# The last product of a float32 chain by seven products of halves within each group of 504 tokens, in place of eight; its output copies all on ScalarE; a new written order

## The chip, the core and the metric

The kernel runs on one core of one Trainium2 chip. The time is the device time of one execution in microseconds (us), the median of the runs. The five engines are TensorE (PE in the rows; its weight loads are shown apart as PEld), VectorE (DVE), ScalarE (ACT), GpSimd (POOL) and SyncE (SP), whose queue issues nearly all DMAs.

## What is computed

Attention over 4 batches of 576 positions and 8 heads, as a sum of a pooled part and a part within a band of 7 positions, gives x (2304 tokens by 512). Two feed-forward stages follow:

```python
def _moe_ref(x, w1, w2, w3, w_out):
    a = x @ w1
    b = x @ w2
    h = a * b @ w3
    return (h @ w_out).astype(np.float32)

def _moe2_ref(x, w1, w2, w3, w_out):
    h = np.maximum(np.maximum(x @ w1, x @ w2), x @ w3)
    return (h @ w_out).astype(np.float32)
```

The change is to the very last product, `h @ w_out` of the second stage: h has 768 features, the output 512.

## The kernel before

**Number format.** Every large product is made three times in the one-pass 32-bit format `fp32r`: both operands are split into a high part (a cast on ScalarE) and a low part (a subtraction on VectorE, `split`, L444 and L446), and `mm3` (L451 to L453) adds low by high, high by low and high by high into one PSUM bank. The product of w3 and w_out (`pw`, L740) is made once in plain float32, ahead of everything.

**Tokens.** The 2304 tokens are cut into four chunks of N = 504 and a rest of 288. Tokens lie in the columns of the moving operand, features in the partitions.

**Stages.** First attention (`down`, `slab`) and the product of weights, mixed; then the first feed-forward stage (`front`, `back`), whose result y goes to DRAM. Then nine units (three pairs of feature blocks by three weight matrices) of the second stage: `halves_front` makes, for two chunks side by side (a group G of 1008 tokens), the product of 2 by 2 blocks with seven products instead of eight (sums of the operands are made ahead by `sums_of_x` and `convert`), keeps the running maximum in `zb` and `area`, and `rest_front` does the 288 tokens plainly. After the third weight matrix the maximum goes to `g_dram[f]`, one array for each of the six feature blocks f.

**The last product.** `final(ch, ...)` loads the six blocks of a chunk (`g_dram`), splits each (`gg`), and makes for each of four output blocks l one PSUM tile by 6 x 3 matmuls of the chunk's width: 72 matmuls a chunk, of 504 columns in four chunks and of 288 in the rest, which comes last. The weights `wm` are three tiles of 1 MB, fetched from `m_dram`. Each PSUM tile is scattered into output tiles by small copies (L1010), half on VectorE and half on ScalarE. An output tile (384 columns) holds one block l of a third of two batches; when its last copy is done, it is sent (192 KB, `out`).

**What sets the order.** Nothing is scheduled at run time. `Program.add` gives every step a number with its dependences; `ORDER` lists for every engine the numbers in the order in which that engine issues them, and the steps are written out so. An engine that waits holds back all that stands behind it in its list. SP's list holds the DMAs: one that waits holds back the others.

Of the kernel before, what the change touches and what calls it, by code (L numbers as in the profile page):

```python
# [96 lines left out]
    "DVE":  # L97
# [38 lines left out]
    "ACT":  # L136
# [231 lines left out]
def attention_moe_kernel(ctx, tc, q0, k0, v0, mask0, ql, kl, vl, mask, qkp, vp, w12, w3t, wo, m123, mo, out):  # L368
# [428 lines left out]
    y_dram = [outside([P, B * S], F32, f"y_dram{l}") for l in range(KX)]  # L797
    g_dram = [outside([P, B * S], F32, f"g_dram{f}") for f in range(NF2)]
    w_dram = [[outside([P, 2048], F32, f"w_dram{u}_{i}") for i in range(2)] for u in range(3 * NF2 // 2)]
    m_dram = [outside([P, 2048], F32, f"m_dram{i}") for i in range(NF2 // 2)]  # L800

# [425 lines left out]
```

## Time and profile before

| what | us |
|---|---|
| median of 3 runs | 756.32 |
| lowest, highest | 754.67, 760.01 |
| the profiled execution | 757.28 |
| its span in the trace | 755.5 |
| TensorE busy in the span | 728.2 |
| VectorE busy | 472.8 |
| ScalarE busy | 315.8 |

The sum of the prediction is made on the profiled execution, which took 0.96 us more than the median of the runs, and 1.8 us more than the span that its trace shows.

### The profile page before, as it was taken

The page shows a single profiled execution, that of the slowest core. Times are in us where ns is not written, and L with a number is a line of the kernel's source. Part 1 is how long each engine was busy: PE and PEld are TensorE (multiplying, and loading weights), DVE is VectorE, ACT ScalarE, POOL GpSimd, SP SyncE. Part 2 cuts the span into 40 slices and gives each one's busy share as a digit, 9 for nine tenths or more (in the row PEclk, how much of TensorE's full clock was granted, in tenths as well). Part 3 has the DMA queues.
Part 4 walks back from the last instruction along what each step waited for, and adds up shares of the span by engine and source line. Part 5 has one row for each costly group of instructions (what it writes and reads, how often), then busy time and mean ns, then how long its engine had stood idle before and what let it go on. Part 6 is the DMA issues. An engine that isn't in the chain of part 4 may idle for free.

```text
span 755.5 us, 15650 instructions
## 1 busy us (share of the span) xinstructions
PE 728.2 (96%) x6404; PEld 572.8 (76%) x6404; DVE 472.8 (63%) x859; ACT 315.8 (42%) x704; POOL 48.3 (6%) x114
## 2 busy tenths in 40 slices
PE   3998999999999999999999999999999999999997
PEld 1445467777877778777888899878887888888886
DVE  5999997776334632343277699978855663475322
ACT  6755495655625743421335356432221220214412
POOL 3210020103020210000000000000000000000000
PEclk9997999999999999999999999999999999999999
DMA  9989565023431331113267586867884265554425
GB/s 322 301 228 306 149 174 152 14 72 78 112 91 44 91 61 34 39 45 101 85 224 262 196 284 243 279 235 276 306 281 147 91 245 198 217 181 145 128 89 198
DMA packets 63191, 126.99 MB, mean 168 GB/s; under 512 B 23376, under 2 KB 43856, under 8 KB 60432
## 3 DMA queue, kind: packets, MB, share of 16 engines
q1 hardware_dynamic: 58512, 122.45, 48.6%
q0 software_dynamic: 4608, 3.55, 3.3%
q8 instruction: 50, 0.82, 0.4%
q14 instruction: 21, 0.17, 0.1%
HBM read 87.43 MB, written 38.54 MB: 167 GB/s over the span
## 4 chain that ended last, share of the span: by engine, by line
PE 86%; DVE 6%; DMA 5%; issue 2%; ACT 0%; SPq 0%; ACTq 0%; DVEq 0%
PE pb L451 11%; PE pb L452 11%; PE pb L453 10%; PE pf L451 9%; PE pf L453 9%; PE pf L452 9%; PE py L451 5%; PE pw L740 5%; PE py L452 4%; PE py L453 4%; PE poq L678 3%; PE sq L633 2%; DMA raw<-w3t 2%; DMA wu<-w_dram 1%; PE po L579 1%
## 5 line engine op out<-in xcount | busy, mean ns | idle before, releaser
L451 PE MATMUL pb<-xc,wu 128*128 128x504 f32 (+1 forms) x324 | 120.7, 373 | 3.1 <-ACT t L906 1.7
L451 PE MATMUL pf<-xt,w 128*128 128x504 f32 (+1 forms) x320 | 120.3, 376 | 0.0
L453 PE MATMUL pb<-xc,wu 128*128 128x504 f32 (+1 forms) x324 | 119.7, 370 | 0.0
L452 PE MATMUL pb<-xc,wu 128*128 128x504 f32 (+1 forms) x324 | 119.7, 369 | 0.0
L452 PE MATMUL pf<-xt,w 128*128 128x504 f32 (+1 forms) x320 | 118.9, 372 | 0.0
L453 PE MATMUL pf<-xt,w 128*128 128x504 f32 (+1 forms) x320 | 118.9, 371 | 0.0
L451 PEld LDWEIGHTS pb<-xc,wu 128*128 128x128 f32 x324 | 60.8, 188 | 17.8 <-DVE t L904 4.3
L451 PEld LDWEIGHTS pf<-xt,w 128*128 128x128 f32 x320 | 60.1, 188 | 11.6 <-ACT dp L572 1.1
L740 PE MATMUL pw<-wf 128*128 128x512 f32 x128 | 64.2, 652 | 4.6 <-DVE wf L477 4.6
L453 PEld LDWEIGHTS pb<-xc,wu 128*128 128x128 f32 x324 | 60.9, 188 | 10.1
L452 PEld LDWEIGHTS pb<-xc,wu 128*128 128x128 f32 x324 | 60.9, 188 | 9.8
L453 PEld LDWEIGHTS pf<-xt,w 128*128 128x128 f32 x320 | 60.1, 188 | 10.3
L452 PEld LDWEIGHTS pf<-xt,w 128*128 128x128 f32 x320 | 60.2, 188 | 9.9
L904 DVE TENSOR_TENSOR t<-t,pb 128x504 f32<-128x504 f32 x60 | 40.4, 677 | 41.7 <-PE pb L453 28.2
L906 ACT COPY t<-pb 128x504 f32<-128x504 f32 x36 | 20.9, 582 | 105.9 <-PE pb L453 102.2
L451 PE MATMUL py<-g,wp 128*128 128x504 f32 (+1 forms) x160 | 64.0, 400 | 0.0
L452 PE MATMUL py<-g,wp 128*128 128x504 f32 (+1 forms) x160 | 59.5, 372 | 0.0
L453 PE MATMUL py<-g,wp 128*128 128x504 f32 (+1 forms) x160 | 59.5, 372 | 0.0
L772 DVE TENSOR_TENSOR z<-pf,z 128x504 f32<-128x504 f32 (+1 forms) x40 | 25.4, 636 | 49.9 <-PE pf L453 38.6
L740 PEld LDWEIGHTS pw<-wf 128*128 128x128 f32 x128 | 25.4, 208 | 33.7 <-issue 27.1
L452 PE MATMUL pb<-gg,wm 128*128 128x504 f32 (+1 forms) x120 | 44.6, 372 | 0.0
L451 PE MATMUL pb<-gg,wm 128*128 128x504 f32 (+1 forms) x120 | 44.4, 370 | 0.0
(117 smaller groups left out, 1191.0 us busy)
## 6 DMA issues: line engine op xcount, KB each, us to landing
wu<-w_dram SPq DMA_DIRECT2D x18, 1024.0 KB, 7.8
w_dram<-hl SPq DMA_DIRECT2D x20, 512.0 KB, 4.7
qk<-qkp SPq DMA_DIRECT2D x16, 576.0 KB, 4.3
raw<-m SPq DMA_DIRECT2D x18, 512.0 KB, 3.8
raw<-w3t SPq DMA_DIRECT2D x16, 512.0 KB, 8.2
raw<-w SPq DMA_DIRECT2D x16, 512.0 KB, 7.2
w_dram<-hls SPq DMA_DIRECT2D x16, 512.0 KB, 4.1
area<-g_dram SPq DMA_DIRECT2D x24, 252.0 KB, 2.7
```

Of the source, the lines that this page charges most:

```text
L451: nc.tensor.matmul(o, wlo, xhi, start=first, stop=False, skip_group_check=again)
L452: nc.tensor.matmul(o, whi, xlo, start=False, stop=False, skip_group_check=again)
L453: nc.tensor.matmul(o, whi, xhi, start=False, stop=last, skip_group_check=again)
L579: e.matmul(po()[a * D:(a + 1) * D, :GD], vd()[:, k, a * D:(a + 1) * D], pt()[:, k, a], start=(k == 0), stop=(k == 1),)
L633: e.matmul(sps[a]()[j * 32:(j + 1) * 32, (half * HP + hp) * BK:(half * HP + hp + 1) * BK], q[h, t:t + 32], k[h, t:t + BK], start=True, sto ...
L678: e.matmul(pos[hp]()[a * D:(a + 1) * D, i * BQ:(i + 1) * BQ], vw()[h, a, i], pt().rearrange("p a n -> p (a n)")[h, c:c + BQ], start=True, ...
L740: e.matmul(os[i](), w()[:, i * P:(i + 1) * P], o(), start=n == 0, stop=n == NF - 1)
L772: prog.add(psum(n), lambda e, pp=pp: e.tensor_tensor(z()[:, :n], pp()[:, :n], z()[:, :n], op=ALU.mult), [pp], [z])
L904: prog.add(dve(N), lambda e: e.tensor_tensor(ap(o), ap(x), ap(y), op=op), [x, y], [o])
L906: copy = lambda o, x: prog.add(act(N), lambda e: e.copy(ap(o), ap(x)), [x], [o])
```

## The change

For each of the four chunks of 504 tokens, `final` now takes the chunk as two halves of 252 columns, the six feature blocks as two halves of three, and the four output blocks as two halves of two, and makes the 2 by 2 block product with seven products. A product has 2 x 3 x 3 = 18 matmuls of 252 columns, so a chunk has 126. Six sums of operands are needed: four are made of g in every chunk, on VectorE (L1029 of the changed kernel), and those of the weights once in `convert`; seven operands of 756 columns are split for each chunk (`go`), and five additions of 504 columns (L1054) and two copies (L1056) put the products together. So `m_dram` and `wm` double to six tiles of 1 MB. The rest of 288 tokens is still made plainly, but ahead of the four chunks (`final_rest`), and in the ninth unit `rest_front` comes ahead of the two groups. Output tiles now hold two blocks l (384 KB each, 12 instead of 24), and all copies into them are on ScalarE (`put`, L982). All five lists of `ORDER` are new.

```diff
-    "12 307 21 23 308 39 116 309 25 310 117 48 50 66 311 312 52 77 75 93 313 79 127 314 151 104 102 152 106 129 "
+    "12 307 23 21 116 39 308 309 25 310 117 50 48 66 311 312 52 75 77 93 79 313 127 151 104 314 102 152 106 129 "
...
-    def convert(srcs, sums, hl, to):
+    def convert(srcs, blocks, hl, to):
...
-        two = [(cv, to[0])]
-        if sums:
-            sm = cvr.tile([P, 1024], F32, "cv")
...
+        sm = cvr.tile([P, 1024], F32, "cv")
+        a11, a12, a21, a22 = ((cv, i) for i in blocks)
...
+    def put(src, t0, n, ls, stride):
+
+        runs = {}
+        for m in range(t0 // TT, (t0 + n) // TT):
...
+        for (b, s, h), (u0, i0, ni) in runs.items():
...
+            prog.add(("ACT", 0.09 + 0.0019 * len(ls) * ni * TT), lambda e, o=o[0], u0=u0, i0=i0, ni=ni, b2=b2, odd=odd: e.copy(
+                view(o(), ls[0] % 2 * T + b2 * NC + 2 * i0 + odd, [[T, len(ls)], [2, ni], [BC, TT]]),
+                view(src(), u0 * TT, [[stride, len(ls)], [2 * TT, ni], [1, TT]])), [src], [(o[0], (b, s, h, i0, ls[0]))])
+            if o[1] == 2 * T:
+                dma(lambda rd=rd, j=j, h=key[2]: out[rd * NJ + j, 2 * h:2 * h + 2].rearrange("l p t -> p l t"),
+                    lambda o=o[0]: o(), [o[0]], [], P * T * 8)
...
-                    cost = (act if h else dve)(ni * TT)
-                    prog.add(cost, lambda e, h=h, o=o[0], c0=c0, ni=ni, b2=b2, i0=i0, odd=odd, pp=pp: (e.copy if h else e.tensor_copy)(
...
+    def final(ch, stage, ops, temps, ms):
+        prog.group += 1
+        n = N // 2
+        b1x, b2x = (stage.tile([P, HF, N], F32, "gf") for _ in range(2))
...
+        def product(j, i, x, pp, first):
+
+            def products(e):
+                for u in range(2):
+                    c = slice(u * P, (u + 1) * P)
+                    for f in range(HF):
+                        w = ms[f][j]()
+                        mm3(pp()[:, u * n:(u + 1) * n], w[:, i, 0, c], w[:, i, 1, c], x()[:, 0, f], x()[:, 1, f],
+                            first and f == u == 0, f == HF - 1, u == 1 or not first)
...
+        x11 = keep(b11)
+        x22 = keep(b22)
+        tt(b22, b22, b12, ALU.subtract)
+        tt(b12, b12, b11, ALU.subtract)
+        v1 = keep(b12)
+        tt(b11, b22, b11, ALU.add)
+        v2 = keep(b11)
+        v3 = keep(b22)
+        x21 = keep(b21)
+        tt(b21, b21, b11, ALU.subtract)
+        v4 = keep(b21)
+        low, high, t0 = [0, 1], [2, 3], ch * N
+        product(0, 0, x11, b1, True)
+        copy(t1, b1)
...
+        product(0, 3, v4, b4, True)
+        add(u3, u3, b4)
+        put(u3, t0, n, high, n)
+        product(0, 2, x21, b1, False)
+        put(b1, t0, n, low, n)
...
+        if u == len(b_units) - 1:
+            rest_front(units[u], w, zs[2], p)
...
-    for ch in range(NW):
-        final(ch, g_places[ch % 3], stage_g, ms)
+    ms = [[fetch(p, d, "wm") for p, d in zip(at, ds)] for at, ds in zip(
+        ((place[4], place[7]), (stage[1], place[8]), (place[6], place[1])), m_dram)]
...
+    for ch in range(NW - 1):
+        final(ch, stage_g, ops, temps, ms)
```

Three places show how instructions stand now.

TensorE near the start, in the stretch in which attention slabs and the product of weights alternate, before the change (`ptq` transposes, `sq` scores of a slab, `pp` and `po` pooled attention, `poq` the slab's values, `pw` the product of weights):

```order
L740 MATMUL pw<-wf 128x512 x4
L633 MATMUL sq<-area 32x32 x32
L569 MATMUL pp<-ident,e 72x72 x8
L633 MATMUL sq<-area 32x32 x16
L633 MATMUL sq<-k,q 32x32 x16
L579 MATMUL po<-dp,area 64x144 x4
L678 MATMUL poq<-pt,area 64x24 x64
```

The same stretch of TensorE's list in the changed kernel:

```order
L633 MATMUL sq<-area 32x32 x32
L569 MATMUL pp<-ident,e 72x72 x4
L740 MATMUL pw<-wf 128x512 x4
L569 MATMUL pp<-ident,e 72x72 x4
L633 MATMUL sq<-area 32x32 x16
L633 MATMUL sq<-k,q 32x32 x16
L579 MATMUL po<-dp,area 64x144 x4
L678 MATMUL poq<-pt,area 64x24 x64
```

A run of four products of weights, which stood ahead of the small matmuls, stands now between the two runs of scores.

TensorE in the changed kernel where the ninth unit ends and the last product begins (`xc` and `wu` are operands of the unit, `gg` the split rest, `wm_6979` the first of the six weight tiles):

```order
L451 MATMUL pb_7090<-xc_5511,wu_6819 128x504
L452 MATMUL pb_7090<-xc_5511,wu_6819 128x504
L453 MATMUL pb_7090<-xc_5511,wu_6819 128x504
L451 MATMUL pb_7161<-gg_7002,wm_6979 128x288
L452 MATMUL pb_7161<-gg_7002,wm_6979 128x288
L453 MATMUL pb_7161<-gg_7002,wm_6979 128x288
```

Before, the unit ended with its rest of 288 columns and chunk 0 of 504 followed; now the second group ends it, and the 72 matmuls of the rest stand between the unit and the first chunk.

ScalarE at the end of its list in the changed kernel, from the first copy that reads the last product's PSUM tile (`pb_7831`) on (`area` and `out` are output tiles, `t` sums of products in SBUF):

```order
L982 COPY out_7397<-pb_7831 128x24
L982 COPY out_7315<-pb_7831 128x24
L982 COPY out_7397<-pb_7831 128x2x2x12
L982 COPY area_7243<-t_7987 128x2x8x12
L982 COPY area_7243<-t_7987 128x24
L982 COPY out_7312<-pb_7831 128x24
L982 COPY out_7397<-t_7744 128x2x3x12
L982 COPY out_7312<-pb_7831 128x2x8x12
L982 COPY out_7315<-pb_7831 128x2x8x12
L982 COPY out_7315<-t_7744 128x2x7x12
L982 COPY out_7315<-t_7932 128x2x4x12
L982 COPY out_7397<-t_7932 128x2x4x12
```

Twelve copies with 1152 elements a partition stand behind the last matmul, and four output tiles wait for them; before, a few copies of the rest's last block stood there, shared between two engines.

## Rows read from the trace of the kernel before

**Rows 1.** The page: span and busy time of the engines.

```profile
span 755.5 us, 15650 instructions
PE 728.2 (96%) x6404; PEld 572.8 (76%) x6404; DVE 472.8 (63%) x859; ACT 315.8 (42%) x704; POOL 48.3 (6%) x114
```

**Rows 2.** Stretches: busy PE, PEld, DVE, ACT, POOL; granted clock; DMA share, GB/s.

```profile
60.00:75.00 15.00, 12.09 (x216) 7.17 (x216) 13.36 (x24) 6.13 (x9) 0.00 (x0) 0.66 0.96 305
75.00:652.90 577.90, 574.25 (x5312) 461.54 (x5311) 364.26 (x635) 239.21 (x505) 31.60 (x68) 1.00 0.48 155
675.30:740.90 65.60, 65.60 (x290) 54.09 (x289) 27.13 (x83) 21.11 (x75) 0.00 (x0) 1.00 0.40 120
740.90:750.60 9.70, 9.66 (x73) 9.40 (x71) 2.54 (x11) 2.10 (x11) 0.00 (x0) 1.00 0.74 271
750.60:755.50 4.90, 0.00 (x0) 0.00 (x0) 0.72 (x4) 0.42 (x2) 0.00 (x0) 0.90 0.51 189
740.50:743.50 3.00, 3.00 (x23) 2.91 (x22) 0.00 (x0) 0.52 (x3) 0.00 (x0) 1.00 0.99 368
```

**Rows 3.** Timeline of TensorE: first matmuls of both widths, and the very last.

```profile
675.33 0.40 PE L451 MATMUL pb<-gg,wm 128*128 128x504 f32 x1
...
740.93 0.29 PE L451 MATMUL pb<-gg,wm 128*128 128x288 f32 x1
...
750.27 0.29 PE L453 MATMUL pb<-gg,wm 128*128 128x288 f32 x1
```

**Rows 4.** Timeline: two weight loads after a pause at 359, two at 741 us.

```profile
358.97 0.19 PEld L451 LDWEIGHTS pf<-xt,w 128*128 128x128 f32 x1
359.08 0.19 PEld L452 LDWEIGHTS pf<-xt,w 128*128 128x128 f32 x1
...
740.93 0.19 PEld L452 LDWEIGHTS pb<-gg,wm 128*128 128x128 f32 x1
741.06 0.19 PEld L453 LDWEIGHTS pb<-gg,wm 128*128 128x128 f32 x1
```

**Rows 5.** Groups by form, VectorE: busy us, mean ns; idle before and its end.

```profile
L446 DVE TENSOR_TENSOR xc<-area,xc 128x1008 fp32r<-128x1008 f32 x14 | 16.6, 1203 | 0.2
L446 DVE TENSOR_TENSOR gg<-area,gg 128x504 fp32r<-128x504 f32 x24 | 16.0, 680 | 13.7 <-ACT gg L444 13.7
L904 DVE TENSOR_TENSOR t<-t,pb 128x504 f32<-128x504 f32 x60 | 40.4, 677 | 41.7 <-PE pb L453 28.2 <-ACT t L906 10.0 <-issue 2.4
```

**Rows 6.** Groups by form, ScalarE.

```profile
L444 ACT CAST xc<-area 128x1008 fp32r<-128x1008 f32 x14 | 14.3, 1038 | 4.3 <-DVE xc L446 1.6 <-PE py L453 1.5 <-PE pf L453 1.2
L444 ACT CAST gg<-area 128x504 fp32r<-128x504 f32 x24 | 14.0, 618 | 24.1 <-DMA area<-g_dram 24.1
```

**Rows 7.** Timeline of ScalarE: eight output copies in a row.

```profile
737.40 1.68 ACT L1010 COPY area<-pb 128x96 f32<-128x96 f32 x8 [3.08 <-DVE area L1010]
```

**Rows 8.** DMA issues from 600 us on: count, KB, median us to landing.

```profile
out<-area SPq DMA_DIRECT2D x24, 192.0 KB, 2.0
wm<-m_dram SPq DMA_DIRECT2D x3, 1024.0 KB, 8.1
```

**Rows 9.** The chain that ended last: its last piece.

```profile
751.67 0.14 DVE area L1010
```

**Rows 10.** Timeline of TensorE near the start, with idle time before and its end.

```profile
14.45 5.09 PE L740 MATMUL pw<-wf 128*128 128x512 f32 x8 [2.54 <-DVE wf L477]
...
54.41 3.60 PE L740 MATMUL pw<-wf 128*128 128x512 f32 x8
...
61.50 1.31 PE L678 MATMUL poq<-pt,area 30*64 30x24 f32 x49 [0.62 <-DVE s L641]
65.08 1.32 PE L678 MATMUL poq<-pt,area 30*64 30x24 f32 x75 [2.27 <-issue]
66.33 6.44 PE L740 MATMUL pw<-wf 128*128 128x512 f32 x8
```

More of the change, by code (lines that the diff above doesn't have):

```diff
@@ L799, in attention_moe_kernel @@
     w_dram = [[outside([P, 2048], F32, f"w_dram{u}_{i}") for i in range(2)] for u in range(3 * NF2 // 2)]
-    m_dram = [outside([P, 2048], F32, f"m_dram{i}") for i in range(NF2 // 2)]
+    m_dram = [[outside([P, 2048], F32, f"m_dram{i}_{j}") for j in range(2)] for i in range(NF2 // 2)]
     HF = NF2 // 2
     A11, A12, A21, A22, S1, S2, S3, S4 = range(8)
-    def convert(srcs, sums, hl, to):
+    def convert(srcs, blocks, hl, to):
         prog.group += 1
@@ L818, in convert @@
         at = lambda t, i: t()[:, i * 256:(i + 1) * 256]
-        two = [(cv, to[0])]
-        if sums:
-            sm = cvr.tile([P, 1024], F32, "cv")
-            for o, x, y, op in ((0, (cv, 2), (cv, 3), ALU.add), (1, (sm, 0), (cv, 0), ALU.subtract),
-                                (2, (cv, 0), (cv, 2), ALU.subtract), (3, (cv, 1), (sm, 1), ALU.subtract)):
-                prog.add(dve(256), lambda e, o=o, x=x, y=y, op=op: e.tensor_tensor(at(sm, o), at(*x), at(*y), op=op),
-                         [x[0], y[0]], [sm])
-            two.append((sm, to[1]))
-        for src, d in two:
+        sm = cvr.tile([P, 1024], F32, "cv")
+        a11, a12, a21, a22 = ((cv, i) for i in blocks)
+        for o, x, y, op in ((0, a21, a22, ALU.add), (1, (sm, 0), a11, ALU.subtract),
+                            (2, a11, a21, ALU.subtract), (3, a12, (sm, 1), ALU.subtract)):
+            prog.add(dve(256), lambda e, o=o, x=x, y=y, op=op: e.tensor_tensor(at(sm, o), at(*x), at(*y), op=op),
+                     [x[0], y[0]], [sm])
+        for src, d in ((cv, to[0]), (sm, to[1])):
             for h in range(2):
@@ L967, in attention_moe_kernel, with load_g, final_rest @@
     outs = {}
-    def final(ch, gplaces, stage, ms):
+    def put(src, t0, n, ls, stride):
+        runs = {}
+        for m in range(t0 // TT, (t0 + n) // TT):
+            q, h = divmod(m, 2)
+            run = runs.setdefault((q // (NSL * NI), q // NI % NSL, h), [m - t0 // TT, q % NI, 0])
+            run[2] += 1
+        for (b, s, h), (u0, i0, ni) in runs.items():
+            rd, b2 = divmod(b, NB2)
+            odd, j = divmod(2 * s + h, NJ)
+            key = rd, j, ls[0] // 2
+            if key not in outs:
+                outs[key] = [Tile(out_places[rd].pop(0), [P, 2, T], F32, "out"), 0]
+            o = outs[key]
+            o[1] += len(ls) * ni * TT
+            prog.add(("ACT", 0.09 + 0.0019 * len(ls) * ni * TT), lambda e, o=o[0], u0=u0, i0=i0, ni=ni, b2=b2, odd=odd: e.copy(
[4 more added lines that the diff above has]
+                    lambda o=o[0]: o(), [o[0]], [], P * T * 8)
+    def load_g(t, at, f, ch):
+        n = WIDTHS[ch]
+        dma(lambda: at(t), lambda: g_dram[f]()[:, ch * N:ch * N + n], [(g_dram[f], ch)], [(t, f)], P * n * 4)
+    def final_rest(ch, gplaces, stage, ms):
         prog.group += 1
@@ L973, in final @@
         for f in range(NF2):
-            st = stage.tile([P, N], F32, "gf")
-            dma(lambda st=st, f=f: st()[:, :n], lambda f=f: g_dram[f]()[:, ch * N:ch * N + n], [(g_dram[f], ch)], [st], P * n * 4)
+            st = stage.tile([P, n], F32, "gf")
+            load_g(st, lambda st: st(), f, ch)
             if f % 2 == 0:
-                g.append(Tile(gplaces[f // 2], [P, 2, 2, N], F32R, "gg"))
+                g.append(Tile(gplaces[f // 2], [P, 2, 2, n], F32R, "gg"))
             t = g[-1]
-            split(lambda t=t, f=f: t()[:, f % 2, 0, :n], lambda t=t, f=f: t()[:, f % 2, 1, :n], lambda st=st: st()[:, :n], n, [st], t)
+            split(lambda t=t, f=f: t()[:, f % 2, 0], lambda t=t, f=f: t()[:, f % 2, 1], lambda st=st: st(), n, [st], t)
         for l in range(KX):
@@ L986, in products @@
                     for f in (2 * f2, 2 * f2 + 1):
-                        c = slice(l * P, (l + 1) * P)
-                        w = ms[f2]().rearrange("p b h n -> p (b h n)")
-                        wp = lambda h: view(w, f % 2 * 1024 + l // 2 * 512 + h * 256 + l % 2 * P, [[1, P]])
-                        mm3(pp()[:, :n], wp(0), wp(1), g[f2]()[:, f % 2, 0, :n], g[f2]()[:, f % 2, 1, :n], f == 0, f == NF2 - 1)
-                prog.add(mm(n, 6), products, [ms[f2], g[f2]], [pp], chain="x")
-            first = ch * N // BQ
@@ L994, in final @@
-            runs = []
-            for q in range(first, first + n // BQ):
-                b, s, i = q // (NSL * NI), q // NI % NSL, q % NI
-                if runs and runs[-1][:2] == (b, s):
-                    runs[-1] = runs[-1][:4] + (runs[-1][4] + 1,)
-                else:
-                    runs.append((b, s, (q - first) * BQ, i, 1))
-            for b, s, c0, i0, ni in runs:
-                rd, b2 = divmod(b, NB2)
-                for h in range(2):
-                    odd, j = divmod(2 * s + h, NJ)
-                    if (rd, j, l) not in outs:
-                        outs[rd, j, l] = [Tile(out_places.pop(0), [P, T], F32, "out"), 0]
-                    o = outs[rd, j, l]
-                    o[1] += ni * TT
-                    cost = (act if h else dve)(ni * TT)
-                    prog.add(cost, lambda e, h=h, o=o[0], c0=c0, ni=ni, b2=b2, i0=i0, odd=odd, pp=pp: (e.copy if h else e.tensor_copy)(
-                        view(o(), b2 * NC + 2 * i0 + odd, [[2, ni], [BC, TT]]), view(pp(), c0 + h * TT, [[BQ, ni], [1, TT]])),
-                        [pp], [(o[0], (b, s, i0))])
-                    if o[1] == T:
-                        dma(lambda rd=rd, j=j, l=l: out[rd * NJ + j, l], lambda o=o[0]: o(), [o[0]], [], P * T * 4)
@@ new lines, in products, with tt, keep, add @@
+                        c = slice(l % 2 * P, (l % 2 + 1) * P)
+                        w, i = ms[f % HF][0](), f // HF * 2 + l // 2
+                        mm3(pp()[:, :n], w[:, i, 0, c], w[:, i, 1, c], g[f2]()[:, f % 2, 0], g[f2]()[:, f % 2, 1], f == 0, f == NF2 - 1)
+                prog.add(mm(n, 6), products, [ms[2 * f2 % HF][0], ms[(2 * f2 + 1) % HF][0], g[f2]], [pp], chain="x")
+            put(pp, ch * N, n, [l], 0)
+    def final(ch, stage, ops, temps, ms):
+        prog.group += 1
+        n = N // 2
+        b1x, b2x = (stage.tile([P, HF, N], F32, "gf") for _ in range(2))
+        for t, k in ((b1x, 0), (b2x, 1)):
+            for f in range(HF):
+                load_g(t, lambda t, f=f: t()[:, f], k * HF + f, ch)
+        b11, b12, b21, b22 = ((t, h) for t in (b1x, b2x) for h in range(2))
+        ap = lambda x: x[0]()[:, :, x[1] * n:(x[1] + 1) * n]
+        def tt(o, x, y, op):
+            prog.add(dve(HF * n), lambda e: e.tensor_tensor(ap(o), ap(x), ap(y), op=op), [x[0], y[0]], [o[0]])
+        def keep(x):
+            w = ops.tile([P, 2, HF, n], F32R, "go")
+            split(lambda: w()[:, 0], lambda: w()[:, 1], lambda: ap(x), HF * n, [x[0]], w)
+            return w
+        b1, b2, b3, b4 = (Tile(everywhere, [P, 512], F32, "pb") for _ in range(4))
+        t1, u2, t5, u3 = (temps.tile([P, N], F32, "t") for _ in range(4))
+        def product(j, i, x, pp, first):
+            def products(e):
+                for u in range(2):
+                    c = slice(u * P, (u + 1) * P)
+                    for f in range(HF):
+                        w = ms[f][j]()
+                        mm3(pp()[:, u * n:(u + 1) * n], w[:, i, 0, c], w[:, i, 1, c], x()[:, 0, f], x()[:, 1, f],
+                            first and f == u == 0, f == HF - 1, u == 1 or not first)
+            prog.add(mm(n, 18), products, [x, *(m[j] for m in ms)], [pp], chain="x")
+        flat = lambda x: x()[:, :N]
+        def add(o, x, y):
+            prog.add(dve(N), lambda e: e.tensor_tensor(flat(o), flat(x), flat(y), op=ALU.add), [x, y], [o])
+        copy = lambda o, x: prog.add(act(N), lambda e: e.copy(flat(o), flat(x)), [x], [o])
+        x11 = keep(b11)
[12 more added lines that the diff above has]
+        copy(t1, b1)
+        product(1, 0, v1, b3, True)
+        copy(t5, b3)
+        product(1, 1, v2, b2, True)
+        add(u2, t1, b2)
+        product(1, 3, x22, b3, False)
+        add(u2, u2, b3)
+        put(u2, t0 + n, n, low, n)
+        product(1, 2, v3, b2, False)
+        add(u3, t1, b2)
+        add(t5, u3, t5)
+        put(t5, t0 + n, n, high, n)
+        product(0, 3, v4, b4, True)
[3 more added lines that the diff above has]
+        put(b1, t0, n, low, n)
@@ L1047, in converted @@
         p, w = b_units[u]
-        convert([m123[w, p], m123[w, p + HF]], True, hl, w_dram[u])
+        convert([m123[w, p], m123[w, p + HF]], range(4), hl, w_dram[u])
     for n in range(len(a_units) + LAG):
@@ L1115, in attention_moe_kernel @@
         fetch_s(u + 1)
-    ms = [fetch(p, d, "wm") for p, d in zip([a_places[len(b_units) % 2], s_place, stage[1]], m_dram)]
-    out_places = [p for s in (*last, *kq, place[11]) for p in parts(s, 5, T)]
-    stage_g = Ring(parts(vws[0], 4, N))
-    g_places = [[place[i] for i in p] for p in ((6, 7, 8), (2, 3, 9), (0, 5, 1))]
-    for ch in range(NW):
-        final(ch, g_places[ch % 3], stage_g, ms)
+    prog.group += 1
+    ms = [[fetch(p, d, "wm") for p, d in zip(at, ds)] for at, ds in zip(
+        ((place[4], place[7]), (stage[1], place[8]), (place[6], place[1])), m_dram)]
+    halved = lambda slots: [p for s in slots for p in parts(s, 2, 2 * T)]
+    out_places = [tqr.slots + halved([last[1], stage[0]]), gr.slots + cvr.slots + halved([last[0]])]
+    final_rest(NW - 1, [*tqr.slots, place[2]], Ring(x32r.slots + odr.slots[1:]), ms)
+    stage_g = Ring([vws[0], place[3], place[10], place[2]])
+    ops, temps = Ring([place[9], place[0], *kq, place[5], place[11]]), Ring(zr.slots + orr.slots + loose + z_slots)
+    for ch in range(NW - 1):
+        final(ch, stage_g, ops, temps, ms)
     order = prog.order()
```

5 lines of the change are left out of this document (3 added, 2 removed), and 206 rows, old and new, of the table ORDER.

## Prediction, made before the changed kernel ran

> **What bounds the kernel now.** I read the page's first part first: TensorE is busy for 728.2 of 755.5 us, VectorE for 472.8, ScalarE for 315.8 [rows 1]. The windows by stage say where the other 27 us are. From 75 to 652.9 us TensorE works 574.25 of 577.90 us, and over the four chunks of the last product 65.60 of 65.60; over the rest's matmuls it works 9.66 of 9.70; then comes a stretch of 4.90 us without a matmul [rows 2]. So the gaps lie ahead of 75 us and behind the last matmul, which ends at 750.27 + 0.29 = 750.56 [rows 3]. In between, TensorE's instructions are the time, as long as the others keep up: a matmul less there is its pitch less. Ahead of 75 us the granted clock is a second matter: 0.66 of full speed on average from 60 to 75, between the levels of 1.2 and 2.4 GHz, and 1.00 from 75 on [rows 2].
>
> **The last product: fewer columns.** The first matmul of 504 columns starts at 675.33, the first of 288 at 740.93 [rows 3]. Between them stand 4 x 72 = 288 matmuls, so one takes 65.60 / 288 = 0.2278 us. From 740.93 to the last start at 750.27 there are 71 steps of 288 columns, 0.1315 us each. The line through both has 0.446 ns a column and gives 0.1155 us for 252 columns; no row has an fp32r matmul so narrow. A chunk took 72 x 0.2278 = 16.40 us and takes 126 x 0.1155 = 14.55. That is 1.85 less in each of four chunks, **-7.4 us**; the rest's 72 x 0.1315 = 9.47 us only move. The term hangs on the pitch: 4 x 126 = 504 matmuls turn each 10 ns into 5.0 us.
>
> Can weight loads be hidden under 252 columns? With 288 columns loads are busy 9.40 of 9.70 us [rows 2], which looks nearly full. But a load is shown 0.19 us long while the next starts 0.13 after it, and after a pause two start 0.11 apart [rows 4]: loads overlap each other, so their busy time is no floor. I keep 0.1155, with the 0.1315 of 288 columns as the bad end: 126 x 0.1315 = 16.57 us a chunk, which gives the whole gain back. The Trainium skill ("Trainium Kernel Development and Optimization", Best Practices) says to judge by the load's busy share and not by the matmul's; by that rule the rest is already bound by loads and 252 columns gain nothing, so that the sum would be that of the rival on loads below. The same skill ("TensorE: Matmul & The Clock Gate", the part on LDWEIGHTS) prices a load by its columns at 1.2 GHz, an estimate of 107 ns for 128; by it loads fit under 115 ns, and the sum stays as it is. The spacing of 0.11 us [rows 4] agrees with the second.
>
> **Do VectorE and ScalarE keep up?** VectorE's split takes 0.680 us for 504 columns and 1.203 for 1008 [rows 5], so 0.94 for 756. A chunk needs seven splits and four sums of 756 (10.3 us) and five additions from PSUM at 0.677 (3.4): 13.7 us in 14.55 of TensorE's. That is tight: before, VectorE had 27.13 of 65.60 [rows 2]. ScalarE casts 504 in 0.618 and 1008 in 1.038 [rows 6], so 756 in 0.83: seven are 5.8 us. Two copies of 504 are at most 1.2. All output copies are now its own: eight of them with 648 elements a partition took 1.68 us [rows 7], 2.6 ns an element, so 2016 elements a chunk are 5.2 us. Together 12.3 of 14.55. The first chunk's operands can be made while TensorE does the rest (9.47 us), which needs little of either engine (2.54 and 2.10 us) [rows 2]. I take **0**; a lead of 9 us shared by four chunks covers waits of a microsecond or two. If the cover is gone, TensorE follows VectorE at 13.7 plus a semaphore's delay at each of seven products; I put that at +1 a chunk, +4.
>
> **The seam.** Twice the weights are six fetches of 1 MB instead of three, at 8.1 us from issue to landing [rows 8]. The last of them takes a place that the ninth unit reads to its end, so it waits on SP's queue for TensorE, and the last stores and the loads of later chunks stand behind it. It is first needed after the rest and one product of 18 matmuls: 9.47 + 2.08 = 11.5 us after the seam, 3.4 more than the landing takes. **0**, and +3 if other transfers slow it. Moving the rest ahead is what buys this: its matmuls are the cover.
>
> **The tail.** Now the last copy ends 751.67 + 0.14 = 751.81 [rows 9], 1.25 us behind the last matmul, and 3.69 us of output and closing follow to 755.5. In the changed kernel twelve copies with 1152 elements stand behind the last matmul on ScalarE alone: at 2.6 ns, 3.0 us; +1.75. Behind the copies go outputs of 384 KB where 192 KB land in 2.0 us [rows 8]. At the 368 GB/s of the busiest stretch [rows 2] 384 KB take 1.07 us, 0.53 more than 192. The last copy completes one output and the copy before it another, so two share the rate at the very end: +0.5 to +1.1. I take **+2.5**. Bounds: +1, if half of the copies can run before the last matmul ends; +4, if all six outputs of the second half of the batches queue up (6 x 1.07 = 6.4 us from the first that is done).
>
> **The new order ahead of 75 us.** In 60 to 72 us TensorE idled 0.62 us before `poq` on VectorE, and 2.27 before a later `poq` that the trace ends with "issue"; then `pw` x8 took 6.44 us, where the same eight took 3.60 at 54.41 [rows 10]. So 0.62 + 2.27 + 2.84 = 5.7 us are to be had there. Eight records in a row of the trace are four `pw` of the order. The change puts a run of four between the two runs of `sq` instead of ahead of both. That puts 3.6 us of dense work into a stretch of small matmuls; it may shorten waits for VectorE's results and keep the clock up. Nothing says that it removes them: the wait that ends in "issue" stands amid small instructions that stay as they are. And a `pw` waits for VectorE's operands too, 2.54 us at 14.45 [rows 10]. I take **-2**, a third, with -5.7 and +2.5 (one more wait like that at 14.45) as ends.
>
> **Sum** on the profiled execution of 757.28 us: -7.4 + 2.5 - 2.0 = -6.9, so 750.4; the profiled execution took 0.96 more than the median of the runs, so **749.4**, 0.9% less than before. About 1% (7.6 us) is what a measurement of this kernel can tell from no change, so the forecast sits on that edge.
>
> **Rivals.**
> *The start is mended in full.* If the moved run fills the waits of 60 to 72 and the clock stays up, -5.7 replaces -2: 745.7. For it: all five lists are new, so more may have moved there than the run that I name. Against: the small matmuls that precede the wait are the same.
> *Loads set the pitch.* 0.1315 at 252 columns: 4 x (16.57 - 16.40) = +0.7 replaces -7.4, so 757.5. For it: 9.40 of 9.70 us busy; against: loads 0.11 apart [rows 4]. This is the result that the skill's first rule above would give.
> *The supply or the seam is late.* +4 from VectorE's 13.7 of 14.55 us, or +3 from the last weight tile: 753.4. For it: VectorE's own work fills 94% of a chunk and its list has no slack for a wait on TensorE. Against: the lead of the rest.
> *A narrow fp32r product runs at the plain float32 rate* (slower than before). `pw` is plain float32, and four of 512 columns took 3.60 us [rows 10], 0.90 each, four times the fp32r rate of 0.2278 [rows 3]. If 252 columns were too few for the fast pass, one would take 0.90 x 252 / 512 = 0.443, a chunk 55.8 us, and the whole 4 x (55.8 - 16.40) = +158 in place of -7.4: 914. For it: no row of before shows the format under 288 columns. Against: from 504 to 288 the pitch falls in proportion. It decides early: with the other terms as they are, a pitch above 0.1155 + 6.9 / 504 = 0.129 us already makes the kernel slower than before.
> *The start gets worse.* Two more waits like that at 14.45 (5.1) and eight `pw` more at the low clock (2.8) replace the -2: about +6, so 757.4.
>
> **How the numbers follow.** Chances: the forecast 0.50 (its own range 746.5 to 753, from the tail's bounds and a start between -4 and 0), the start mended 0.22, supply or seam late 0.12, loads 0.08, the plain rate 0.05, the start worse 0.03. The range from 744 to 758 takes in all but the plain rate and outliers of the others. Faster by over 1% means under 748.8: nearly all of the mended start, and two fifths of the forecast: 0.43. Slower by over 1% means above 763.9: the plain rate, and tails of supply and start: 0.10. Within 1%: 0.47.
>
> **What the changed kernel's profile would show.** The pitch: 18 matmuls of a product in 2.08 us from first start to the next product's first. The supply: in the windows of the four chunks TensorE without idle time, and no wait on `go`; VectorE near 13.7 us a chunk. The seam: no wait for a DMA on `wm` after the rest. The tail: last matmul to span's end in about 7.4 us instead of 4.95, with ScalarE's copies over 3 us of them. The start: the first dense stretch of full clock reached some 2 us earlier, and fewer than 2.9 us idle at `poq`. The prediction is wrong if the pitch is over 0.12, if a wait on VectorE stands at each product, or if the start moves by over 4 us either way.

## Result and the profile after

| what | us |
|---|---|
| before, median of 4 runs | 756.54 |
| after, median of 4 runs (745.3 to 747.4) | 746.49 |
| ratio, 95% interval | 0.9861 (0.9822 to 0.9900) |
| predicted | 749.4 (744 to 758) |

The changed kernel is 1.4% faster; its time lies within the predicted range and 2.9 us below the predicted value. The profiled execution took 747.40 us with a span of 745.6, 9.9 less than before [rows 1].

The page of the changed kernel, span and busy time of the engines:

```profile
span 745.6 us, 16119 instructions
...
PE 718.1 (96%) x6620; PEld 576.9 (77%) x6620; DVE 505.8 (68%) x853; ACT 341.0 (46%) x744; POOL 47.4 (6%) x114
```

TensorE's busy time falls by 10.1 us although it has 216 matmuls more. Where the gain is along the program is read from a few starts. TensorE's timeline in the changed kernel: the first `pf` of the first stage, the first matmul of the rest (288 columns), the first of a chunk (252), and the last of all:

```profile
102.42 0.50 PE L451 MATMUL pf<-xt,w 128*128 128x504 f32 x1
...
669.39 0.29 PE L451 MATMUL pb<-gg,wm 128*128 128x288 f32 x1
...
678.93 0.28 PE L451 MATMUL pb<-go,wm 128*128 128x252 f32 x1
...
737.38 0.28 PE L453 MATMUL pb<-go,wm 128*128 128x252 f32 x1
```

The same `pf` before, in its own timeline:

```profile
104.54 0.50 PE L451 MATMUL pf<-xt,w 128*128 128x504 f32 x1
```

With the starts of [rows 3] the span splits into four pieces:

| piece | before | after | difference | forecast |
|---|---|---|---|---|
| start, to the first `pf` | 104.54 | 102.42 | -2.1 | -2.0 |
| first `pf` to the last product | 570.79 | 566.97 | -3.8 | 0 |
| last product, to the end of its last matmul | 75.23 | 68.27 | -7.0 | -7.4 |
| tail, from there to the end of the span | 4.94 | 7.94 | +3.0 | +2.5 |
| sum | 755.5 | 745.6 | -9.9 | -6.9 |

Windows of the changed kernel (columns as in [rows 2]): all from 75 us to the last product, the rest, the four chunks, the tail, and six microseconds of it.

```profile
75.00:669.40 594.40, 593.03 (x5413) 479.59 (x5414) 387.63 (x681) 250.80 (x526) 32.02 (x71) 1.00 0.52 168
669.40:678.90 9.50, 9.50 (x73) 9.50 (x72) 7.57 (x11) 3.93 (x6) 0.00 (x0) 1.00 0.78 294
678.90:737.60 58.70, 58.70 (x506) 58.56 (x504) 47.12 (x59) 39.28 (x104) 0.00 (x0) 1.00 0.37 122
737.70:745.60 7.90, 0.00 (x0) 0.00 (x0) 0.00 (x0) 2.33 (x12) 0.00 (x0) 0.65 0.83 299
738.00:744.00 6.00, 0.00 (x0) 0.00 (x0) 0.00 (x0) 2.03 (x10) 0.00 (x0) 0.68 1.02 368
```

Over the rest and the four chunks TensorE has no idle time. In the tail DMA is full from 738 to 744 us at 368 GB/s. The first row answers to the 574.25 of 577.90 us of [rows 2]: 3.65 us idle then (and 0.08 more in the 22.4 us from the end of that window to the last product), 1.37 now. This is the piece that the forecast left at zero. What TensorE waited for from 100 us on, before the change (total us, times, longest):

```profile
PE pb L451 <- ACT t L906: 1.7, 1, 1.7
PE pb L451 <- DMA wu<-w_dram: 0.8, 1, 0.8
```

and in the changed kernel:

```profile
PE pb L451 <- DVE t L902: 0.5, 1, 0.5
```

Besides these, both have one wait of 0.5 to 0.7 us that the trace ends with "issue".

### The profile page after: what moved, and what is told of

The parts are those of the page before. It is cut to its first block, busy times and chain, and to the rows that moved or that the text cites. A ratio compares the mean times of both kernels' runs of the same rounds, so it can differ in the third digit from the quotient of the medians.

```text
span 745.6 us, 16119 instructions
## 1 busy us (share of the span) xinstructions
PE 718.1 (96%) x6620; PEld 576.9 (77%) x6620; DVE 505.8 (68%) x853; ACT 341.0 (46%) x744; POOL 47.4 (6%) x114
## 4 chain that ended last, share of the span: by engine, by line
PE 88%; DVE 6%; DMA 3%; issue 1%; ACT 1%; SPq 0%; ACTq 0%; DVEq 0%
PE pb L451 11%; PE pb L453 11%; PE pb L452 11%; PE pf L451 9%; PE pf L452 9%; PE pf L453 9%; PE py L451 5%; PE pw L740 5%; PE py L452 5%; PE py L453 4%; PE poq L678 2%; PE sq L633 2%; PE po L579 1%; DVE wf L477 1%; DVE wf L475 1%
## 5 line engine op out<-in xcount | busy, mean ns | idle before, releaser
L451 PE MATMUL pb<-go,wm 128*128 128x252 f32 x168 | 46.9, 279 | 0.0
L453 PE MATMUL pb<-go,wm 128*128 128x252 f32 x168 | 46.8, 279 | 0.0
```

What stands on the lines that cost most here:

```text
L451: nc.tensor.matmul(o, wlo, xhi, start=first, stop=False, skip_group_check=again)
L453: nc.tensor.matmul(o, whi, xhi, start=False, stop=last, skip_group_check=again)
```

## Experiments

Line numbers in several of these kernels are four lower: there L447 to L449 are `mm3`, L674 is `poq`, L736 `pw` and L1050 the additions. A run without an interval is a single execution.

### The kernel before once more, and the new order alone

> The kernel before, profiled a second time, to see which of its gaps come back. Theory 1: the gaps belong to the order of the steps, so the 2.27 us on TensorE that the first profile ends with 'issue', the low clock behind it (0.66 from 60 to 75 us) and the waits of 0.84 and 1.74 us at 495 and 568 us all stand here again, within 0.3 us. Theory 2: the 2.27 us is a chance of that one execution; then it is under 0.5 us here, the first matmul pf starts 2 us earlier, and the forecast's term for the start was read from an accident.

The kernel took 757.41 us in this one run. Its timeline has the wait again, longer, and its first `pf` 1.1 us earlier than the first time:

```profile
64.95 1.32 PE L678 MATMUL poq<-pt,area 30*64 30x24 f32 x75 [2.76 <-issue]
...
103.42 0.50 PE L451 MATMUL pf<-xt,w 128*128 128x504 f32 x1
```

So the wait is no accident (theory 1, though not within the 0.3 us that it set), but the clock behind it is not fixed: 0.77 over 60 to 75 us here against 0.66 [rows 2]. The two waits of the second stage stand at the same instructions with other sizes, 1.4 us on DMA and 0.5 on ScalarE against 0.8 and 1.7 in the first profile, 1.9 against 2.6 in all.

The second kernel keeps the old last product and takes the steps that both kernels share, up to the weights' last conversion, in the new order:

```diff
 ORDER, numbers below 2021 (every step ahead of the weights' last conversion), all five engines:
-    their places filled in the old relative order
+    the same places filled in the new relative order
```

> The kernel before with its old last product and old tail; only the steps up to the weights' last conversion, which both kernels have in common, are put in the new relative order on all five engines. Theory 1 (the order is worth 2.1 us at the start and 3.8 us between the start and the seam, whatever the last product is): 756.5 - 5.9 = 750.6 us, last product of the old length 75.2 us. Theory 2 (the gain between start and seam comes with the new last product's surroundings, such as the rest of the ninth unit that now stands ahead of its groups): only the start's 2.1 us show, 754.4 us. Theory 3 (the order gives nothing by itself): 756.5 us.

It took 750.25 us against 755.66 of the kernel before beside it, ratio 0.9926 (0.9900 to 0.9952): 5.4 us, theory 1. Its first `pf` starts at 101.39. The second stage, by windows, in the kernel before, the changed one and this one:

```profile
467.90:675.30 207.40, 204.33 (x973) 169.76 (x973) 140.15 (x218) 53.70 (x91) 0.00 (x0) 1.00 0.64 225
```

```profile
464.90:669.40 204.50, 203.73 (x975) 170.12 (x974) 149.89 (x242) 56.75 (x97) 0.00 (x0) 1.00 0.72 255
```

```profile
463.50:667.90 204.40, 203.80 (x974) 170.04 (x974) 141.56 (x220) 53.62 (x91) 0.00 (x0) 1.00 0.65 228
```

TensorE's idle time falls from 3.07 us to 0.77 and 0.60, and the stage by 2.9 and 3.0. In the first and the third of these kernels TensorE's own order of this stage is the same; the lists of VectorE, ScalarE and SP differ. The gain does not need the new last product: of the 10 us, 5.4 come with the order of the shared steps, and the seven products bring the rest, 7.0 us less the 3.0 of the longer tail.

### The start: one run moved, and moved back

The prediction named one run of four `pw`. Here it moves alone in the kernel before, and then alone back in the changed kernel:

```diff
-PE: 127 314 151 104 102 152
+PE: 127 151 104 314 102 152
```

> The kernel before with one step moved: the run of four pw that stood ahead of the small matmuls near 54 us now stands between the two halves of the eight pp. Theory 1 (the forecast's mechanism: this one move fills the wait and keeps the clock): the 2.27 us wait at poq is under 0.3 us, the eight pw behind it take about 4.5 us instead of 6.44, and the first pf starts about 2 us earlier than in the kernel before. Theory 2 (the gain at the start comes from the many other moves, VectorE's list above all): the wait stays over 1.5 us and the first pf starts within 0.5 us of the kernel before.

> The changed kernel with the one run of four pw put back ahead of the small matmuls, where it stood before; all else of the new order stays. Theory (the wait of 2 to 3 us at poq is TensorE's own instructions, which arrive late when many small matmuls stand in a row; the 16 KB transfer on the instruction queue falls into it): the wait is back, over 1.5 us, that transfer falls within it, and the first pf is 1 to 3 us later than in the changed kernel (102.0 to 102.5). Rival (the wait goes by VectorE's lists, which stay new here): no such wait, first pf within 0.5 us.

Timeline of TensorE in the kernel before with the run moved:

```profile
52.71 0.65 PE L655 MATMUL ptq<-ident,s 128*128 128x128 f32 x4
...
55.41 1.25 PE L565 MATMUL pp<-ident,e 72*72 72x72 f32 x4 [1.35 <-ACT e L556]
56.45 5.30 PE L736 MATMUL pw<-wf 128*128 128x512 f32 x8
...
63.78 1.82 PE L674 MATMUL poq<-pt,area 30*64 30x24 f32 x128
...
76.70 3.70 PE L736 MATMUL pw<-wf 128*128 128x512 f32 x8 [1.61 <-DVE wf L473]
...
104.59 0.50 PE L447 MATMUL pf<-xt,w 128*128 128x504 f32 x1
```

The wait ahead of `poq` is gone, and the granted clock over 60 to 75 us is 1.00. But the low clock has only moved ahead: from 56.4 to 59.8 us the granted clock is 0.50, and the eight `pw` there take 5.30 us. Nothing is gained: 1.35 us now go to ScalarE's `e` and 1.61 to VectorE's `wf`, and the first `pf` starts at 104.59, where it was at 104.54 and 103.42. The kernel took 756.30 us. Each theory is right in one half: the wait goes, as theory 1 has it, and the first `pf` stays, as theory 2 has it. In the changed kernel with the run put back:

```profile
52.37 0.60 PE L655 MATMUL ptq<-ident,s 128*128 128x128 f32 x4
...
62.65 1.33 PE L674 MATMUL poq<-pt,area 30*64 30x24 f32 x76 [1.36 <-issue]
...
101.65 0.49 PE L447 MATMUL pf<-xt,w 128*128 128x504 f32 x1
```

The wait is back, 1.36 us where over 1.5 was expected, and the first `pf` is no later than in the changed kernel (102.42; 101.97 in its second profile); 747.16 us. The run's place decides about this wait. What the wait is worth, the first `pf` alone does not tell, because the profiles scatter by two microseconds already ahead of the moved run. The last step that stands ahead of it in every list is this `ptq`, here in the kernel before and in the changed one:

```profile
53.92 0.66 PE L659 MATMUL ptq<-ident,s 128*128 128x128 f32 x4
```

```profile
54.70 0.60 PE L659 MATMUL ptq<-ident,s 128*128 128x128 f32 x4
```

| lists and place of the run | profiles | `ptq` starts | first `pf` | between |
|---|---|---|---|---|
| old, run in its old place | 3 | 53.92 to 54.43 | 103.42 to 104.80 | 48.99 to 50.62 |
| old, run moved | 1 | 52.71 | 104.59 | 51.88 |
| new, run moved | 9 | 52.84 to 54.70 | 100.59 to 102.68 | 47.71 to 48.46 |
| new, run put back | 1 | 52.37 | 101.65 | 49.28 |

From the `ptq` on, the means are 50.0 us with the old lists and 48.0 with the new ones, and this is the 2 us of the start. With the run put back the new lists need 49.3, 0.8 us more than the longest of the nine profiles: the run's place is worth about 1.3 us there. It does not show in the first `pf` because this one profile reached the `ptq` earlier than all others, which the edit cannot have caused. In the old lists the same move costs time, since other operands come late. So the move gains only together with the other new lists. Each direction rests on a single profile.

What the wait is, the DMA view suggests. Kernel before, 62.5 to 65.2 us:

```profile
q1 hardware_dynamic: 468, 0.92, 97.2%
q0 software_dynamic: 43, 0.03, 7.5%
q8 instruction: 1, 0.02, 2.1%
```

Changed kernel, 56.5 to 58.5 us:

```profile
q8 instruction: 1, 0.02, 2.9%
```

A transfer on the instruction queue falls into the wait before; in the changed kernel one runs in the dense `pw` ahead, and from 62 to 66 us there is none. In the second profile of before it falls into the wait again, and with the run put back it stands in the 2.7 us before the wait's end. That TensorE's instructions come late amid many small matmuls fits all of these, but no run changed the transfer by itself.

The changed kernel with its first 601 steps in the old order was to price the start as a whole:

```diff
 ORDER, numbers below 601, all five engines:
-    their places filled in the new relative order
+    the same places filled in the old relative order
```

> The changed kernel with its first 601 steps (first attention and the product of weights) back in the old relative order on all engines; all else as changed. Theory 1 (start and middle are separate terms): the first pf starts 2.1 us later, near 104.6 us, and the whole takes 746.5 + 2.1 = 748.6 us, with stages and seam as in the changed kernel. Theory 2 (delays at the start are absorbed by waits later on): the first pf is later, but the seam is not, and the whole stays within 0.5 us of 746.5.

The first `pf` starts at 104.80, as both theories have it, but the kernel took 771.83 us: the crossed lists hold back later steps (TensorE waits 6.2 us for ScalarE's `e` and 5.2 for VectorE's `s` in the first stage). It says nothing about what is absorbed later. For the start it agrees with the others (it is one of the three profiles in the first line of the table): with old lists the first `pf` stands at 103.4 to 104.8 in four profiles, with new ones at 100.6 to 102.7 in ten.

### Is the new pitch that of columns or of loads?

```diff
-  mm3(pp()[:, u * n:(u + 1) * n], ..., x()[:, 0, f], x()[:, 1, f], ...)
+  m = 128 if f else n
+  mm3(pp()[:, u * n:u * n + m], ..., x()[:, 0, f, :m], x()[:, 1, f, :m], ...)
```

> The changed kernel, with 12 of the 18 matmuls of each product of the last stage cut from 252 to 128 columns (the first three of each half of the output stay whole); the same weights are loaded. It leaves out part of the sums. Theory 1 (252 columns are bound by columns, loads have slack): the cut matmuls follow each other by 128 x 0.446 = 57 ns, or by whatever floor the loads have, and that floor is well under 0.115 us. Theory 2 (at 252 columns the load of the weights already sets the pitch, as its busy share of 61.96 in 62.10 us would say): the cut matmuls keep 0.115 us, within 3 ns.

TensorE's timeline inside a product, four matmuls cut to 128 columns:

```profile
700.35 0.27 PE L448 MATMUL pb<-go,wm 128*128 128x128 f32 x1
700.46 0.27 PE L449 MATMUL pb<-go,wm 128*128 128x128 f32 x1
700.57 0.28 PE L447 MATMUL pb<-go,wm 128*128 128x128 f32 x1
700.69 0.27 PE L448 MATMUL pb<-go,wm 128*128 128x128 f32 x1
```

From 700.35 to 700.69 there are three steps: 0.113 us each. (All 503 steps of the last product, a third of them still 252 columns wide, average (733.39 - 676.49) / 503 = 0.1131.) With 252 columns the pitch was (737.38 - 678.93) / 503 = 0.1162. Half the columns save 3 ns where columns alone would save 55. By the number set beforehand theory 2 holds (0.113 is within 3 ns of 0.115): there is a floor of 0.11 us under these matmuls, and at 252 columns they stand just above it. That the weight loads set it fits the two loads 0.11 apart [rows 4]; no run changed the loads themselves, so this cause is argued. A limit on how fast TensorE's instructions follow each other it is not: 128 `poq` took 1.82 us above, 0.014 each. Yet at 252 columns the floor costs next to nothing, 0.7 ns between the forecast 0.1155 and the measured 0.1162: the two limits nearly meet at this width. The kernel took 743.47 us, the start's scatter included; the last product fell from 68.27 to 66.70 us.

### What makes the tail

```diff
+    def put(src, t0, n, ls, stride, dv=False):   # dv: e.tensor_copy on VectorE
-        put(b1, t0, n, low, n)
+        put(b1, t0, n, low, n, ch == NW - 2)
```

> The changed kernel with six of the twelve copies behind the last matmul (those that read the last PSUM tile) moved from ScalarE to VectorE, which is idle there. Theory 1 (copies on ScalarE alone make the tail longer): the last copy ends about 1.1 us earlier and the tail from the last matmul to the end of the span falls from 7.9 to about 6.8 us. Theory 2 (six outputs of 384 KB that become ready together make it: 2.36 MB at 366 GB/s are 6.4 us from about 0.3 us behind the last matmul): copies end earlier, the tail stays within 0.4 us of 7.9.

747.17 us. The copies behind the last matmul, on VectorE and on ScalarE:

```profile
737.47 1.12 DVE L978 COPY out<-pb 128x24 f32<-128x24 f32 x6 [1.42 <-PE pb L449]
...
737.58 0.95 ACT L978 COPY out<-t 128x72 f32<-128x72 f32 x4
```

They end at 738.59, against 740.03 in the changed kernel, whose list ends so:

```profile
738.58 0.84 ACT L982 COPY out<-pb 128x192 f32<-128x192 f32 x2
739.19 0.84 ACT L982 COPY out<-t 128x168 f32<-128x168 f32 x3
```

Counted from the end of each kernel's last matmul (737.44 and 737.66), that is 1.15 us against 2.37. The tail did not move: 745.4 less 737.16 + 0.28 is 7.96 us. Copies that end 1.2 us earlier are worth nothing, theory 2. Six outputs of 384 KB are 2.36 MB, 6.4 us at 368 GB/s, and the windows above show DMA full for six microseconds of the tail.

To send three of the six earlier, the last chunk's products were put in other orders:

```diff
-x11 v1 v2 x22 v3 v4 x21
+x11 v1 x21 v2 x22 v3 v4   (first trial, operands too)
+x11 v1 v2 v3 v4 x22 x21   (second and third, operands as before)
```

> The changed kernel with the seven products of the last chunk in another order, so that the three outputs of the lower two blocks are complete two products (4.2 us) before the last matmul, and ScalarE's leftover copies of earlier chunks ahead of the last chunk's; nothing else changes. Theory 2 (the tail is the transfer of six outputs): three are sent under the last products, the tail falls by 1 to 3 us, to 5 to 7. Theory 1 (copies make the tail): it falls by what the copies behind the last matmul become fewer and no more, and the outputs' transfers do not overlap TensorE. Should VectorE's splits come too late in the new order, TensorE waits at the products of the last chunk and the last stage gets longer than 68.3 us.

756.30 us. TensorE waits 4.1 us for ScalarE's `t` and 2.5 for VectorE's `t`, and the last product grows by 11 us. The rest of the growth is the clock: the granted clock is 0.50 from 718.8 to 722.2 and from 732.5 to 739.3 us, each beginning shortly after the end of the 2.5 us wait or within the 4.1 us one. The tail falls only to 7.3. The trial says little beyond that.

> The changed kernel with the last chunk's products in the order x11, v1, v2, v3, v4, x22, x21 (x22 moves behind v4), operands made in the same order as before, ScalarE's leftover copies of earlier chunks ahead of the last chunk's, and the copies behind the last matmul shared by both engines. The three outputs of the upper two blocks are complete two products before the end. Theory 2 (the transfer of outputs that are ready together makes the tail): three outputs of 384 KB go under the last products, three remain behind the last matmul, 1.18 MB or 3.2 us at 366 GB/s in place of 6.4; with copies of 0.8 to 1.2 us and the issue ahead of them the tail falls from 7.9 to between 5.5 and 6.7 us, and the kernel to about 744.6. The other reading of the last experiment but one (TensorE had to wait because ScalarE's or VectorE's list was in another order, not because products were) predicts no wait on TensorE here, last stage 68.3 us; if the order of the products itself costs waits, the last stage is longer by over 2 us again.

> The reordered last chunk of the high-first kernel, with the leftover copies that read PSUM ahead of ScalarE's last cast (so that PSUM banks come free in time), and all copies behind the last matmul on ScalarE. If TensorE's wait of 1.4 us there was for a bank that ScalarE's list freed late, it is gone and the last stage is 68.3 to 68.6 us again; the tail stays near 6.4 us since it is the outputs' transfer; the kernel takes 1.2 to 1.5 us less than the changed one, about 745.2. If the order of the products itself makes the wait, the last stage stays near 69.8 and nothing is gained.

The second trial took 746.98 us, ratio 0.9877 (0.9854 to 0.9899), beside 746.52 of the changed kernel. Its tail is 746.1 - 739.63 = 6.5 us, 1.5 less and within the expected 5.5 to 6.7. The bytes of three outputs would be 3.2 us, but they were ready only shortly before the end. A window of this kernel shows DMA full from 738.5 us on:

```profile
738.50:744.30 5.80, 1.12 (x10) 0.93 (x8) 0.88 (x3) 1.80 (x7) 0.00 (x0) 0.81 1.00 364
```

Only the 1.1 us up to 739.63 lie under the last products, and about as much is saved, as the transfer's theory says. But the last product is 1.6 us longer, by one wait:

```profile
731.03 0.35 PE L447 MATMUL pb<-go,wm 128*128 128x252 f32 x1 [1.38 <-ACT area L978]
```

I took ScalarE at its word and put its PSUM copies earlier in the third. That failed: 749.47 us, ratio 0.9909 (0.9875 to 0.9942), the tail still 6.4 us, and the wait longer and under another name:

```profile
730.50 0.35 PE L447 MATMUL pb<-go,wm 128*128 128x252 f32 x1 [2.54 <-DVE t L1050]
```

`v2` and `v3` share a PSUM tile, and VectorE must read the first sum out of it in between. In the changed kernel `x22` stands there as 2.1 us of cover; with `x22` moved TensorE waits for VectorE, whose list has a split and ScalarE's cast ahead of that sum. VectorE's rows show this for both trials, second and third, whatever releaser the wait is put down to:

```profile
729.35 0.94 DVE L442 TENSOR_TENSOR go<-gf,go 128x756 fp32r<-128x756 f32 x1 [1.48 <-ACT go L440]
730.21 0.67 DVE L1050 TENSOR_TENSOR t<-t,pb 128x504 f32<-128x504 f32 x1
```

```profile
728.81 0.95 DVE L442 TENSOR_TENSOR go<-gf,go 128x756 fp32r<-128x756 f32 x1 [2.64 <-ACT go L440]
729.68 0.67 DVE L1050 TENSOR_TENSOR t<-t,pb 128x504 f32<-128x504 f32 x1
```

The sums end at 730.88 and 730.35, and TensorE goes on 0.15 us behind them, at 731.03 and 730.50. In the third trial the granted clock then falls to 0.50 from 731.6 to 735.0 us, about another 1.7 us. A list with the sum ahead of that split was not run. No version here beats the changed kernel.

> The changed kernel again, beside the reordered one in the same rounds. Theory: 746.5 us, 0.986 of the kernel before within 0.3%; last stage 68.3 us and tail 7.9 us as in its first profile; the first pf between 100.6 and 102.5 us, since the runs so far put that scatter on the start.

The changed kernel beside the second trial: 746.52 us, ratio 0.9869 (0.9846 to 0.9891), first `pf` at 101.97, tail 745.4 - 737.48 = 7.9. It repeats within 0.1 us.

### What covers the seam

```diff
-  for f in (2 * f2, 2 * f2 + 1):
+  for f in (2 * f2, 2 * f2 + 1) if f2 == 0 else ():
```

> The changed kernel with only 24 of the 72 matmuls of the rest of 288 tokens between the ninth unit and the first chunk (it leaves out two thirds of the rest's sums): 48 x 0.1315 = 6.3 us of cover are taken from the seam. Theory 1 (the rest ahead of the chunks hides the last weight fetches and the first operands, as the prediction says): TensorE waits at the first chunk for weights or operands, 2 us or more, and the kernel gains less than 4.3 us. Theory 2 (nothing was hidden, the fetches and operands are ready long before): no wait, the whole 6.3 us are gained, 740.2 us.

744.58 us. The last product fell by 2.7 us of the 6.3 removed. The waits of TensorE from 640 us on:

```profile
PE pb L448 <- DVE go L442: 2.6, 3, 1.4
```

The starts of the chunk's matmuls are 3.6 us late in all; the 2.6 count only from the end that the trace shows for the matmul before. Theory 1, with one correction: it is operands that come late, not weights. The 3.2 us of the rest that are left are too few to prepare the first chunk, where the 9.5 us of the whole rest were enough; no wait on the weight tiles shows even so.

## Why the prediction was right, step by step

- **The pitch.** Forecast 0.1155 us for 252 columns, measured 0.1162; 58.73 us for four chunks (to the end of the last matmul) where 58.2 were forecast. The rest's product moved unchanged, 9.54 against 9.47. The last product as a whole gave 7.0 of the 7.4. The rival on loads was wrong about 252 columns; below them there is a floor, at 0.113 us 3% away. By the Trainium skill's rule to judge by the load's busy share ("Trainium Kernel Development and Optimization", Best Practices) 58.56 of 58.70 us would leave no headroom, and the run with 128 columns agrees. At 288 columns the same rule misled: loads were busy 9.40 of 9.70 us [rows 2], and the pitch still fell by 12%. The same skill's estimate of 107 ns ("TensorE: Matmul & The Clock Gate", the part on LDWEIGHTS) is a little under the measured 113.
- **VectorE and ScalarE keep up.** This held. The groups by form of the changed kernel, from 600 us on, have the interpolated durations nearly to the nanosecond:

```profile
L446 DVE TENSOR_TENSOR go<-gf,go 128x756 fp32r<-128x756 f32 x28 | 26.2, 944 | 6.2 <-ACT go L444 6.0
L1054 DVE TENSOR_TENSOR t<-t,pb 128x504 f32<-128x504 f32 x16 | 10.6, 676 | 5.7 <-PE pb L453 5.7
```

```profile
L444 ACT CAST go<-gf 128x756 fp32r<-128x756 f32 x28 | 22.8, 830 | 18.5 <-DVE gf L1029 8.2 <-PE pb L453 6.6 <-DMA gf<-g_dram 2.7
```

  With 15.1 us of sums (L1029) and 2.7 of additions that read no PSUM, VectorE's work on the four chunks is 54.6 us, 13.7 a chunk as forecast. TensorE did not wait, and the short rest shows how little was left: with 6.3 us less of lead it lost 3.6. The rival's price of 1 us a chunk for delays between the engines stood on no row, and no run shows it; the loss in the short rest lies all in the first chunk.
- **The seam.** No wait, as forecast. The cover was right for the weights, but the part that needs it is the operands.
- **The tail.** +3.0 against +2.5. The mis-sized part is the choice between the bounds: I added copies and two outputs, 1.75 + 0.8, and kept six queued outputs as the bad end. The six are what it is; the copies on ScalarE, 1.75 of my 2.5, cost nothing. They are also shorter than the sum had it, 2.33 us in place of the over 3 that the prediction named as a sign. The bad end of +4 was 1 us too high, since the outputs begin to leave while the copies still run.
- **The start.** -2.1 against -2, but the -2 was a third of what was to be had and not worked out from a mechanism, so the size is luck. The moved run takes the wait at `poq` away, as hoped: 0.86 us idle there where 2.9 stood. The clock it raises in part at most: over 60 to 75 us it was 0.66 and 0.77 in the two profiles of before, and it is 0.89 in the changed kernel, but 0.77 with the new order alone, where the wait is gone too. With the new lists the run's place is worth about 1.3 us, with the old ones alone it loses. Which of the other moves makes the rest is open.
- **Two numbers of the rivals.** The start mended in full would have been 745.7, nearer to 746.49 than the forecast, but it is not what happened: the start gave 2.1 of its 5.7 us. In the rival of a worse start, 5.1 + 2.8 in place of the -2 gives 759.3 and not 757.4, beyond the range.
- **The step that failed.** "In between, TensorE's instructions are the time, as long as the others keep up: a matmul less there is its pitch less" was taken as if nothing else were to be had there. [Rows 2] showed 3.65 us idle in that stretch, and the new lists removed most of it: -3.8 us where the forecast had zero, more than the whole error of 2.9. The number came within 2.9 us because the last product and the tail, 0.4 and 0.5 us worse than forecast, took part of it back. The share of it that is idle time in the second stage is 2.3; the rest is spread over starts a fraction of a microsecond apart and was not traced further.

## What to carry to other kernels

Before a new order is priced, add up the bound engine's idle time over the whole program, also where a stage looks dense: half a percent of a long stage is as much as the stall that catches the eye. At the end of a kernel ask when the first of the last outputs can leave and how many bytes follow, not how long the last copies take. A stall that is named in the trace is worth its length only if nothing else is late behind it: run the one move by itself before the gain is credited to it, in the old lists and in the new, and measure from the last step that the move cannot have touched.

## What was not expected of the hardware

Where every matmul loads its own 128 columns of weights, one of 128 columns in this format follows the one before it after 0.113 us, one of 252 after 0.116: narrower tiles than 252 columns save almost nothing. And the releaser named in a wait's row can be another than the one that matters: two orders of the same last chunk wait for the same sum of VectorE under two names, ScalarE's `area` and VectorE's `t`.
